# A copy of one column of zeros as ScalarE's first operation, in causal attention followed by a gated MLP

## The chip, the cores and the metric

The kernel runs on one core of one Trainium2 chip. The metric is the device time of the program in microseconds. A profile is one execution with the hardware profiler on; its span runs from the first to the last recorded work, and the execution's own time is a little longer.

## The reference

Attention over 8 batches, 8 heads, 576 positions and 64 values a head, with a mask that is causal by blocks of 64; then the heads are put side by side as `x` of 4608 x 512 and go through a gated MLP without an activation function:

```python
scores = scale * np.matmul(q, k.transpose(0, 1, 3, 2))     # scale = 1 / sqrt(64)
scores = np.where(block_i >= block_j, scores, -1000000000.0)
scores = scores - np.max(scores, axis=-1, keepdims=True)
attn = np.exp(scores)
attn = attn / (np.sum(attn, axis=-1, keepdims=True) + 1e-09)
attn_out = np.matmul(attn, v)
...
a = x @ w1
b = x @ w2
h = a * b @ w3
return h @ w_out
```

## The kernel before, in words

Two heads of one batch make a pair; there are 32 pairs (`NN`), and the transposed q and k of a pair fill 128 partitions, 64 for each head. The weights come as 64-bit numbers and are put together on the chip from two 32-bit halves (`assemble`, L161 to L172: one ScalarE operation, L168, then three VectorE operations, L169 to L171). The products `w3 @ w_out` are formed once on the chip (`gen_product`, L461), so that the MLP has two stages: the gated one (L481) and the output one (L499).

The work falls into three parts. The opening (L124 to L529) prepares the first pair. Pairs 0 to 3 (`EARLY`) run attention while the weights arrive, are put together and multiplied; their score tiles are L281, their exponentials L289, their products with v L321. From pair 4 on, attention of one pair runs interleaved with the MLP of the tokens that are finished, by hand-written orders (`FIRST_PLANS`, `PLAN`), one letter per step.

The opening goes like this. SP issues the loads of the first pair: k, then q (`load_qk(0)`, L116), the identity matrix (L129), v (L121), and the constants (L138). VectorE sets a tile `cst` of 128 x 1152 to zero (L135), and the two DMAs of L138 write five rows of constants into each half of it. `shift_mask(0)` (L189) casts k to bf16 (`kb`, L192) and q into the block-diagonal `qd` in two halves, the first on VectorE and the second on ScalarE (L194). TensorE then forms bf16 scores from the two (`mx`, L206), VectorE takes their row maxima (`m`, L213), TensorE transposes them (`mt`, L217), ScalarE negates them (`ms`, L219), and SP writes them as rows into the operand tiles `qk` (`shift`, L228). Meanwhile ScalarE casts q and k into `qk` (L251), SP copies them to the other half of the partitions (L255), ScalarE copies zeros and constants from `cst` into the rest of `qk` (L521), SP fetches the first piece of weights (`wraw`, L158), and VectorE forms the low parts (L258). Then the first score tiles (L281) can run.

What sets the order: inside the opening, `manual_schedule` holds PE, VectorE, ScalarE, SP and GpSimd to the order of the program. For pairs 0 to 3 a planner in the framework orders each engine's instructions by priority and its own estimate of times; the attention steps have high priority, the weights fill in. From pair 4 on TensorE's order is the program's. Each engine and each queue works in order. Waits between engines come from the data that the instructions read and write, tile region by tile region. The table load of ScalarE is not in the source: the compiler puts it in ahead of an operation.

Of the kernel before, what the change touches and what calls it, by code (L numbers as in the profile page):

```python
# [7 lines left out]
F32 = mybir.dt.float32  # L8
# [8 lines left out]
P = 128  # L17
# [60 lines left out]
def block_causal_attention__then__gated_mlp_kernel(ctx, tc, qkv, consts, ident_in, w1, w2, w3t, wout, out_t):  # L78
    nc = tc.nc
    w1, w2, w3t, wout = (w.bitcast(I32) for w in (w1, w2, w3t, wout))  # L80

    cpool = ctx.enter_context(tc.tile_pool(name="cpool", bufs=1))
# [50 lines left out]
    tl["early"] = wp  # L133
    cst = wp.tile([P, RQK], F32, tag="rqk", name="cst")
    nc.vector.memset(cst, 0.0)  # L135
    five = [slice(oth[j].start, oth[j].start + 5) for j in range(2)]
    for j in range(2):
        nc.sync.dma_start(out=cst[five[j]], in_=consts)  # L138
# [513 lines left out]
```

## Time and profile before

| | before |
|---|---|
| median of three runs | 965.94 us (965.72 to 966.31) |
| the profiled execution's own time | 964.53 us |
| its span | 962.7 us |
| mean granted TensorE clock | 0.995 of full speed |
| TensorE, VectorE, ScalarE, GpSimd busy | 97%, 63%, 59%, 32% of the span |
| DMA | 111.68 MB, mean 116 GB/s |

Times in the profile are microseconds from the start of the span. PE is TensorE, PEld its weight loads, DVE VectorE, ACT ScalarE, POOL GpSimd, SP the engine that issues the DMAs; a name with q (SPq, ACTq) is an engine's sequencer. A row names a line of the kernel, the operation, the tile written, the tile read, the shape and a count; in brackets stands how long the engine was idle before it and who ended that. The chain of waits is followed back from the last instruction: at each step to what released it.

### The profile page before, as it was taken

The numbers are of one execution on the slowest core, as the hardware profiler recorded it, in microseconds if no ns is written. First come the engines' busy times: TensorE is split into PE (matmuls) and PEld (weight loads), VectorE is DVE, ScalarE is ACT, GpSimd is POOL, SyncE is SP. The second block draws the span as 40 slices with busy tenths as digits, with TensorE's granted clock in tenths as the row PEclk, the third lists the DMA queues.
The fourth block names the chain that finished last, engine by engine and source line by source line (L and its number), as shares of the span: only waits on it lengthen the run. The fifth ranks groups of instructions, "written<-read, shape, count | busy, mean of one in ns | idle before, by whom it ended". The sixth has DMA issues, their size and how long they took to land.

```text
span 962.7 us, 13385 instructions
## 1 busy us (share of the span) xinstructions
PE 936.8 (97%) x4608; PEld 750.4 (78%) x4608; DVE 608.7 (63%) x1289; ACT 565.4 (59%) x1274; POOL 304.4 (32%) x254
## 2 busy tenths in 40 slices
PE   5799979999999999999999999999999999999998
PEld 3355557888888888888888888888888888888886
DVE  5999977766777667766776777767776776210010
ACT  5677666666666666666666667666666665222121
POOL 0000043443345334533443334333443443223120
PEclk9999979999999999999999999999999999999999
DMA  7797333455444554455445544554454442000001
GB/s 255 248 296 236 136 82 94 113 124 145 113 113 114 144 124 113 107 143 118 109 100 142 123 109 112 133 130 107 108 130 125 108 114 60 22 1 33 12 1 44
DMA packets 48823, 111.68 MB, mean 116 GB/s; under 512 B 5866, under 2 KB 14186, under 8 KB 48756
## 3 DMA queue, kind: packets, MB, share of 16 engines
q1 hardware_dynamic: 48756, 110.84, 44.3%
q8 instruction: 36, 0.59, 0.3%
q14 instruction: 31, 0.25, 0.1%
HBM read 50.51 MB, written 9.44 MB: 62 GB/s over the span
## 4 chain that ended last, share of the span: by engine, by line
PE 90%; ACT 4%; DVE 3%; DMA 1%; issue 1%; SPq 0%; POOL 0%; ACTq 0%
PE ab L481 41%; PE o L499 20%; PE s L281 10%; PE x L345 9%; PE mx L206 4%; PE w L461 3%; PE x L321 2%; DMA rqk<-in_qkv 1%; ACT wbits L168 1%; DMA wraw<-in_wout 1%; DVE wbits L170 1%; ACT qk L251 1%; PE tot L362 0%; ACT x L371 0%; PE mt L217 0%
## 5 line engine op out<-in xcount | busy, mean ns | idle before, releaser
L489 POOL TENSOR_TENSOR gl<-a,gh 128x512 fp32r<-128x512 f32 x72 | 93.6, 1300 | 238.7 <-ACT gh L488 238.7
L281 PE MATMUL s<-qk 128*128 128x288 f32 (+4 forms) x768 | 159.8, 313 | 8.7 <-DMA qk<-ms 5.7
L281 PEld LDWEIGHTS s<-qk 128*128 128x128 f32 (+1 forms) x768 | 125.8, 183 | 40.7 <-issue 9.9
L213 DVE TENSOR_REDUCE m<-mx 128x1 f32<-128x512 f32 (+6 forms) x256 | 125.9, 504 | 36.2 <-PE mx L206 34.8
L300 ACT ACTIVATE ph<-s 128x448 fp32r<-128x448 f32 x224 | 86.1, 384 | 70.3 <-PE s L281 63.4
L481 PE MATMUL ab<-xh,w2h 128*128 128x512 f32 x288 | 126.6, 440 | 0.0
L271 POOL TENSOR_TENSOR vs<-rv,vs 128x320 fp32r<-128x320 f32 x56 | 48.8, 871 | 235.5 <-ACT vs L270 235.5
L499 PE MATMUL o<-gh,wh 128*128 128x512 f32 x288 | 117.3, 407 | 0.0
L487 DVE TENSOR_TENSOR a<-ab,a 128x512 f32<-128x512 f32 x72 | 49.6, 689 | 106.7 <-PE ab L481 104.0
L302 DVE TENSOR_TENSOR pl<-s,ph 128x448 fp32r<-128x448 f32 x168 | 81.6, 485 | 54.3 <-ACT s L301 53.8
L481 PE MATMUL ab<-xh,w1h 128*128 128x512 f32 x288 | 114.5, 398 | 0.1
L481 PE MATMUL ab<-xl,w1h 128*128 128x512 f32 x288 | 113.6, 394 | 0.0
L298 DVE TENSOR_TENSOR pl<-rsum,ph 128x288 fp32r<-128x288 f32 x112 | 56.3, 526 | 90.4 <-ACT ph L297 90.2
L481 PE MATMUL ab<-xh,w1l 128*128 128x512 f32 x288 | 113.2, 393 | 0.0
L481 PE MATMUL ab<-xl,w2h 128*128 128x512 f32 x288 | 113.1, 393 | 0.0
L499 PE MATMUL o<-gl,wh 128*128 128x512 f32 x288 | 112.8, 392 | 0.0
L481 PE MATMUL ab<-xh,w2l 128*128 128x512 f32 x288 | 112.8, 392 | 0.0
L499 PE MATMUL o<-gh,wl 128*128 128x512 f32 x288 | 112.6, 391 | 0.0
L243 POOL TENSOR_TENSOR rqk<-rqk,hf 128x1152 fp32r<-128x1152 f32 x27 | 72.2, 2675 | 91.1 <-ACT hf L240 82.6
L303 DVE TENSOR_TENSOR rsum<-s,rsum 128x448 f32<-128x448 f32 x224 | 92.9, 415 | 1.7
L345 PE MATMUL x<-ph,vs 128*128 128x128 f32 x336 | 87.3, 313 | 0.2 <-DVE ph L302 0.2
L301 ACT ACTIVATE s<-s 128x448 f32<-128x448 f32 x224 | 85.7, 382 | 0.0
(76 smaller groups left out, 1743.6 us busy)
## 6 DMA issues: line engine op xcount, KB each, us to landing
qk<-hf SPq DMA_DIRECT2D x108, 288.0 KB, 3.1
rqk<-in_qkv SPq DMA_DIRECT2D x31, 576.0 KB, 4.8
qk<-rqk SPq DMA_DIRECT2D x54, 288.0 KB, 4.8
rv<-in_qkv SPq DMA_DIRECT2D x32, 320.0 KB, 2.8
out_t<-o SPq DMA_DIRECT2D x36, 256.0 KB, 2.0
wraw<-in_w3t SPq DMA_DIRECT2D x8, 1024.0 KB, 6.1
wraw<-in_w SPq DMA_DIRECT2D x8, 1024.0 KB, 7.6
wraw<-in_wout SPq DMA_DIRECT2D x4, 1024.0 KB
```

The costliest lines, as they stand in the source:

```text
L213: nc.vector.reduce_max(m[:, col : col + 1], sc, axis=AX.X)
L243: nc.gpsimd.tensor_tensor(out=lo, in0=rqk_of[n], in1=hf, op=ALU.subtract)
L281: nc.tensor.matmul(t[ks, at : at + q1 - q0], qk[j][:, 2 + s, kr], qk[j][:, s, q0:q1], start=(s == 0), stop=(s == 1))
L298: nc.vector.tensor_tensor(out=low, in0=r, in1=h, op=ALU.subtract)
L300: nc.scalar.activation(h, sc, AF.Exp, scale=SCALE)
L301: nc.scalar.activation(sc, sc, AF.Exp, scale=SCALE)
L302: nc.vector.tensor_tensor(out=low, in0=sc, in1=h, op=ALU.subtract)
L303: nc.vector.tensor_tensor(out=r, in0=sc, in1=r, op=ALU.add)
L345: nc.tensor.matmul(xps[:, to : to + w], v[:, c, :], parts[s][:, a : a + w], start=(u < 2 and s == 0), stop=((u, s) in ((0, 1), (len(PV) - ...
L481: nc.tensor.matmul(acc[i], l[:, c, fs], r[c], start=(c == 0 and s == 0), stop=(c == NC - 1 and s == 2))
L489: nc.gpsimd.tensor_tensor(out=gl[f // 4][:, f % 4], in0=a32, in1=gh[f // 4][:, f % 4], op=ALU.subtract)
L499: nc.tensor.matmul(t, l[:, f, es], r[f // 4][:, f % 4], start=(f == 0 and s == 0), stop=(f == NF - 1 and s == 2))
```

## The change

After the memset of `cst`, ScalarE copies its first column (128 partitions, one element each) into a new tile of one column in the pool `cpool`, which nothing reads. The line stands ahead of the two DMAs that write the constants into `cst`, and ahead of every other ScalarE operation of the program.

```diff
@@ -133,6 +133,7 @@
     tl["early"] = wp
     cst = wp.tile([P, RQK], F32, tag="rqk", name="cst")
     nc.vector.memset(cst, 0.0)
+    nc.scalar.copy(cpool.tile([P, 1], F32, name="table"), cst[:, 0:1])
     five = [slice(oth[j].start, oth[j].start + 5) for j in range(2)]
     for j in range(2):
         nc.sync.dma_start(out=cst[five[j]], in_=consts)
```

## The prediction

> **What bounds the kernel now.** I read the page first, for the engine that fills the span and for the chain that ended last.
>
> ```profile
> span 962.7 us, 13385 instructions
> PE 936.8 (97%) x4608; PEld 750.4 (78%) x4608; DVE 608.7 (63%) x1289; ACT 565.4 (59%) x1274; POOL 304.4 (32%) x254
> PE 90%; ACT 4%; DVE 3%; DMA 1%; issue 1%; SPq 0%; POOL 0%; ACTq 0%
> ```
>
> The reader is to see that TensorE is the kernel: busy for 97% of the span and 90% of the chain. A change to one ScalarE operation can only matter where the chain leaves TensorE. So the next view was the chain of waits, from the start to 30 us.
>
> ```profile
> 0.74 0.40 SPq L116
> ...
> 1.19 3.12 DMA rqk<-in_qkv
> ...
> 4.33 0.02 ACTq L194
> ...
> 4.39 1.28 ACT L194
> ...
> 5.68 0.67 ACT qd L194
> ...
> 8.72 0.60 SPq L255
> ...
> 9.37 5.68 DMA wraw<-in_wout
> ...
> 15.07 1.13 ACT wbits L168
> ...
> 16.55 1.11 PE s L281 x2
> ...
> 18.36 1.49 PE x L321 x2
> ...
> 21.69 0.43 PE mx L206 x2
> ...
> 27.59 0.75 PE x L321 x2
> ```
>
> Columns are start, duration, what. The first 16 us hold no TensorE link at all. The first pair's q and k land at 1.19 + 3.12 = 4.31, ScalarE passes its semaphore at 4.33, and then 1.28 us go to something on line 194 that is not yet the cast of qd: that begins at 5.68. The timeline of the same stretch says what it is.
>
> ```profile
> 1.04 1.02 DVE L135 MEMSET cst<- 128x1152 f32 x1 [1.04 <-PEq L640]
> ...
> 2.60 0.69 SPq L138 DMA_DIRECT2D cst<-in_consts  x2
> ...
> 4.39 1.28 ACT L194 ACT_TABLE_LOAD   x1 [4.39 <-DMA rqk<-in_qkv]
> 4.41 0.74 DVE L194 CAST qd<-rqk 64x576 bf16<-64x576 f32 x1 [0.37 <-DMA rqk<-in_qkv]
> 5.68 0.67 ACT L194 CAST qd<-rqk 64x576 bf16<-64x576 f32 x1
> ...
> 6.40 1.04 PE L206 MATMUL mx<-kb,qd 128*128 128x512 bf16 x2 [6.40 <-ACT qd L194]
> ...
> 7.55 1.77 SPq L255 DMA_DIRECT2D qk<-qk  x2
> ...
> 8.60 2.32 ACT L521 CAST qk<-cst 64x1152 fp32r<-64x1152 f32 x2
> ...
> 11.50 0.27 ACT L219 ACTIVATE ms<-mt 9x128 fp32r<-9x128 f32 x1 [0.57 <-PE mt L217]
> ...
> 15.37 0.82 PE L281 MATMUL s<-qk 128*128 128x288 f32 x2 [2.18 <-DMA qk<-ms]
> ...
> 18.16 1.70 PE L321 MATMUL x<-pe,ve 128*128 128x448 f32 x2
> ...
> 21.53 0.59 PE L206 MATMUL mx<-kb,qd 128*128 128x512 bf16 x2
> ...
> 27.43 0.92 PE L321 MATMUL x<-pe,ve 128*128 128x448 f32 x2
> ```
>
> It is an ACT_TABLE_LOAD that stands behind the wait for the data. ScalarE did nothing in the 4.39 us before, and the load stands in full on the path that releases TensorE's first matmul at 6.40.
>
> **The change part by part.** *The added copy.* It reads one column of cst, so it waits for the memset, which ends at 1.04 + 1.02 = 2.06. No row shows a copy of 128x1. The nearest small ScalarE row is ms at 0.27 us for 9x128; one element a partition should not be dearer, and an instruction costs not less than nothing, so 0 to 0.27, and I take 0.27, as that row is small already. Behind it on ScalarE's queue stands everything else of that engine, none of which can start before the data. In the late case the load waits for the memset as it now waits for the data: 2.06 + 1.28 + 0.27 = 3.61. In the early case the load stands ahead of the wait and the copy ends at 2.06 + 0.27 = 2.33. Both are before 4.31, with 0.70 us to spare in the worse. The cover is ScalarE's idle time; if it were gone, the copy would cost its 0.27 at most.
>
> *The load that moves.* Line 194's cast on ScalarE can begin where the load began, at 4.39, instead of 5.68: 1.29 us earlier. It then ends at 4.39 + 0.67 = 5.06. What is late next is VectorE's half of qd, at 4.41 + 0.74 = 5.15: TensorE needs both. Its first matmul came 0.05 after the ScalarE half (5.68 + 0.67 = 6.35, then 6.40), so it comes at 5.20, and that path gains 1.20. The other path, the two casts of L251, the two DMAs of L255 and the first weight fetch behind them on SP, gains the whole 1.29: the fetch goes out at 9.37 - 1.29 = 8.08 and lands near 13.8, where ScalarE takes it up for wbits. The paths meet at about 16 us: TensorE's second score tile (15.37, behind the row of maxima) carries 1.20, ScalarE's wbits (15.07) carries 1.29. The later one counts: 1.20.
>
> A page speaks for more than this: the Trainium skill, page "ScalarE: Activation LUTs", section "What ACT_TABLE_LOAD costs", gives 1283 ns for the load and some 1380 ns of drain, 2.66 us per switch. The trace agrees with the load alone: the cast starts 0.01 us after it ends. By the page the sum would be 2.66.
>
> All that stands between the landing and the cast is 5.68 - 4.31 = 1.37, so the direct gain has that for its upper end. Its lower end is zero, if the load does not move.
>
> *The wait that is added.* The copy reads all 128 partitions of column 0 of cst, and the two DMAs of L138 then write ten rows of it, that column too. They must now wait for the copy. They went out at 2.60; now at 2.60 (early case) or 3.61 (late case). Behind them on SP's queue stands nothing until L255, at 7.55 before and 6.26 now, and two issues at 0.69 together end at 4.30: SP is not held up. Who needs the constants is L521, at 8.60 before and 7.31 now. Landing time for 22.5 KB is not shown; the nearest row is the far larger load of rqk, 0.74 to 4.31, 3.57 us from issue. By that they land at 4.30 + 3.57 = 7.87 at worst, 0.56 late; the 0.57 us that ScalarE stands idle before ms hides this. Cost nothing; if the cover is gone, 0.56.
>
> The new tile of one column adds bytes to a pool but no instruction. Other queues are not passed.
>
> *Whether it lasts to the end.* Everything from 6.40 on waits for something that came from this first chain, not for a fixed time, so it moves as a block.
>
> ```profile
> 50.00:66.00 16.00, 16.00 (x58) 8.62 (x58) 16.00 (x22) 11.74 (x19) 0.00 (x0) 1.00 0.86 268
> ...
> 200.00:300.00 100.00, 100.00 (x535) 84.31 (x534) 68.91 (x162) 65.03 (x158) 39.41 (x33) 1.00 0.49 119
> ```
>
> In these windows (from:to, length, then busy time of PE, weight loads, VectorE, ScalarE, GpSimd, clock, DMA share, GB/s) TensorE is busy throughout: work that starts earlier is done earlier, and there is no gap that could take the gain back. Sum: -1.20, within -1.37 and 0.
>
> The profiled execution took 964.53 us, its span of 962.7 and 1.83 around it. From it the change gives 963.33. The three timed runs have their median at 965.94, 1.41 above, and as the forecast is for such runs I put 965.94 - 1.20 = 964.74, say 964.7. About 0.2%, 1.93 us, is what a measurement of this kernel can tell from no change: the forecast is below that.
>
> **The rivals.** *The clock at the start* (faster or less fast). On the chain the two products of 448 columns at 18.36 took 1.49 us, those at 27.59 0.75 (the timeline's rows from 18.16 and 27.43 give the form), and the two 512-column products at 21.69 took 0.43 against 1.04 at 6.40. So TensorE ran at half speed until shortly before 21.69. If the rise to full speed stays where it is in absolute time, the 1.20 us won are half-speed time and worth 0.60: 965.3. If it comes earlier by more than the work does, the half-speed stretch in which the chain is TensorE's, from 16.55 to 21.69, shrinks; at the most all of its 5.14 us halve, another 2.57: between 964.0 (where 0.2% begins) and 962.2, some 963.1. Against a large effect speaks that the three runs lie within 0.6 us of each other.
>
> The Trainium skill, page "TensorE: Matmul & The Clock Gate", section "What's actually happening", says that the activity window of 3413 ns runs freely and is not restarted by the kernel. By that rule the rise does not follow the work, and each run would draw its own share; the close times of the runs do not bear that out.
>
> *The other clock dip* (faster).
>
> ```profile
> 130.00:140.00 10.00, 8.50 (x26) 6.59 (x26) 7.31 (x9) 6.19 (x15) 4.88 (x4) 0.51 0.31 93
> ```
>
> Where the stage of the first four pairs ends, the granted clock is 0.51. Should the shifted schedule avoid it, TensorE's 8.50 busy us halve, 4.25 less: 960.5. It has no reason to: what precedes it moves as a block.
>
> *The drain counts too* (faster). A second 1.38 behind the load would go too: 965.94 - 2.66 = 963.3. The 0.01 us between load and cast speaks against it.
>
> *No load moves, or there are two* (same). If the load is placed by the first operation that really needs a table, or one set serves the copy and another Abs and Exp, the first cast or wbits still waits 1.28. For one set for all:
>
> ```profile
> L194 ACT ACT_TABLE_LOAD x1 | 1.3, 1283 | 4.4 <-DMA rqk<-in_qkv 4.4
> ```
>
> Before, one load in the whole run came ahead of a cast and served exponentials too. Price: 965.9.
>
> *The planner orders the early pairs otherwise* (slower). After the opening, the orders of VectorE, ScalarE and SP in the first four pairs come from a planner's estimates, and an added ScalarE operation shifts them. The place is a weight piece put ahead of a mask or a low part that TensorE waits for.
>
> ```profile
> L168 ACT ACTIVATE wbits<-wraw x20: 1129/1158/1227, 15.1 to 110.9; 128x1024 f32<-128x1024 f32 x20
> L169 DVE TENSOR_SCALAR wbits<-wbits x20: 653/690/695, 16.2 to 118.0; 128x1024 int32<-128x1024 int32 x20
> L170 DVE SCALAR_TENSOR_TENSOR wbits<-wraw,wbits x20: 1171/1218/1226, 17.0 to 119.3; 128x1024 int32<-128x1024 int32 x20
> L171 DVE SCALAR_TENSOR_TENSOR w<-wraw,wbits x8: 1216/1218/1225, 27.7 to 96.7; 128x1024 int32<-128x1024 int32 x8
> ```
>
> One piece is 1.16 + 0.69 + 1.22 + 1.22 = 4.29 us from ScalarE to VectorE. In front of TensorE it costs 4.29 - 1.20 = 3.09: 969.0. It decides from 3.13 us of new waiting on (1.20 + 1.93). Against it: the copy lies ahead of the first data and moves no estimate that the data set.
>
> **How the numbers follow.** The block shift of 1.20 (964.7): 0.66. Rise of the clock unmoved (965.3): 0.08. Rise earlier still (963.1): 0.10. No gain from the load (965.9): 0.07. Planner (969.0): 0.06. Other dip (960.5): 0.02. Drain (963.3): 0.01. Faster by over 0.2%: 0.10 + 0.02 + 0.01 = 0.13. Slower by as much: 0.06. The same: 0.81. The range goes from 963.2 (the drain case and about half of the earlier rise are in) to 966.2 (no gain, and 0.3 for the spread of the three runs); about 0.13 is left out.
>
> **What would show it.** In the profile after, the table load begins before 2.4 us and there is one of it; the copy of one column ends by 3.61; L194's cast on ScalarE begins at 4.39 and TensorE's first matmul at 5.20, now released by VectorE; the consts' DMAs go out by 3.6 and L521 starts near 7.3; the first weight fetch goes out at 8.1; the order on every engine is as before, and at 200 us all stands 1.2 earlier. The forecast is wrong if the load stays behind the data, if TensorE's first fast matmuls do not come 1.2 earlier, or if a wait between 16 and 130 us appears that was not there.

## The result and the profile after

The changed kernel is slower: 972.85 us, median of six runs (972.45 to 974.57), against 965.5 us for the kernel before beside it (six runs, 961.86 to 966.31). The ratio is 1.0087, 95% interval 1.0077 to 1.0097. The profiled execution took 973.0 us, its span is 971.2. In the code after, the copy is L136, and every line behind it has a number one higher (L195 is the former L194).

The timeline of the opening, after:

```profile
0.73 1.28 ACT L136 ACT_TABLE_LOAD   x1 [0.73 <-PEq L641]
...
2.10 0.19 ACT L136 COPY table<-cst 128x1 f32<-128x1 f32 x1
...
2.60 0.68 SPq L139 DMA_DIRECT2D cst<-in_consts  x2
...
4.42 0.67 ACT L195 CAST qd<-rqk 64x576 bf16<-64x576 f32 x1 [2.13 <-DMA rqk<-in_qkv]
4.43 0.74 DVE L195 CAST qd<-rqk 64x576 bf16<-64x576 f32 x1 [0.35 <-DMA rqk<-in_qkv]
...
5.33 1.01 PE L207 MATMUL mx<-kb,qd 128*128 128x512 bf16 x2 [5.33 <-DVE qd L195]
...
7.34 2.32 ACT L522 CAST qk<-cst 64x1152 fp32r<-64x1152 f32 x2
```

The table load starts with the engine, at 0.73; the copy runs at 2.10, and ScalarE's cast no longer waits for anything but its data. TensorE starts at 5.33 instead of 6.40, released by VectorE's half. The chain of waits after, with the same links as in the prediction:

```profile
4.36 0.02 ACTq L195
...
4.42 0.67 ACT qd L195
...
8.11 5.81 DMA wraw<-in_wout
...
13.94 1.13 ACT wbits L169
...
15.42 1.11 PE s L282 x2
...
17.23 1.49 PE x L322 x2
...
20.53 0.43 PE mx L207 x2
```

The first weight fetch goes out at 8.11 instead of 9.37; the second score step starts at 15.42 instead of 16.55; the fast row-maximum products come at 20.53 instead of 21.69. So far the forecast holds, with 1.1 to 1.3 us won. The loss comes later, and steadily. SP's issues of the first output tile of a block of tokens, in block one and in block six, of the kernel before and then of the changed one (start, duration, line):

```profile
213.12 0.35 SPq L504 DMA_DIRECT2D out_t<-o  x1
...
707.30 0.35 SPq L504 DMA_DIRECT2D out_t<-o  x1
```

```profile
212.45 0.36 SPq L505 DMA_DIRECT2D out_t<-o  x1
...
711.21 0.35 SPq L505 DMA_DIRECT2D out_t<-o  x1
```

At block one the changed kernel is still 0.67 us ahead; five blocks later it is 3.91 behind. That is 4.58 us in five blocks, 0.92 a block, and a block has 288 products of 512 columns in the MLP: 3.2 ns a product, if all of it is theirs. The last stretch of the chain shows it without attention beside it. Before, then after:

```profile
893.60 5.44 PE ab L481 x24
899.08 38.37 PE ab L481 x168
937.46 21.77 PE o L499 x96
```

```profile
900.17 5.60 PE ab L482 x24
905.80 39.47 PE ab L482 x168
945.27 22.41 PE o L500 x96
```

The same 288 products take 5.60 + 39.47 + 22.41 = 67.48 us instead of 65.58. An output product follows the one before it after 22.41 / 96 = 233 ns instead of 21.77 / 96 = 227. TensorE waits for nobody in either; it streams more slowly. Two such blocks cost 3.8 us, seven blocks at 0.92 some 6.4, together 10.2; less the 1.1 of the opening that is 9.1, by this rough sum, where the spans differ by 8.5 us. TensorE's weight loads follow the same order of tiles in both traces, and so do the instructions of the other engines but for the added copy, so no planner's decision is in it.

### The profile page after: what moved, and what is told of

It reads as the page before. It is cut to its first block, busy times and chain, and to the rows that moved or that the text cites. A ratio compares the mean times of both kernels' runs of the same rounds, so it can differ in the third digit from the quotient of the medians.

```text
span 971.2 us, 13356 instructions
## 1 busy us (share of the span) xinstructions
PE 946.2 (97%) x4579; PEld 750.1 (77%) x4608; DVE 608.8 (63%) x1289; ACT 566.1 (58%) x1275; POOL 304.1 (31%) x254
## 4 chain that ended last, share of the span: by engine, by line
PE 90%; DVE 4%; ACT 3%; DMA 2%; issue 1%; SPq 0%; ACTq 0%
PE ab L482 42%; PE o L500 21%; PE s L282 10%; PE x L346 9%; PE mx L207 3%; PE w L462 2%; PE x L322 2%; DVE wbits L171 1%; DMA wraw<-in_w3t 1%; ACT qk L252 1%; DMA wraw<-in_wout 1%; ACT wbits L169 1%; DVE w L172 1%; PE tot L363 0%; DVE m L214 0%
## 5 line engine op out<-in xcount | busy, mean ns | idle before, releaser
L489 ACT CAST gh<-a 128x512 fp32r<-128x512 f32 x72 | 44.3, 616 | 70.3 <-DVE a L488 69.0
```

## The experiments

What the diff does besides the copy: its tile stands behind the weights, identity, `qk` and `qd` in the pool `cpool`, so everything that is allocated later starts 32 bytes (a tile's smallest size in a partition) further on. Among that are `xh`, `xl`, `gh` and `gl`, the moving operands of the MLP. The first theory was that TensorE reads operands more slowly when they start off a round address (A, a multiple of 64); the rivals were the copy or the moved load itself (B), the old place itself or a multiple of 128 (C), and the places of the work tiles. All ratios are to the kernel before on the same chip; its medians in the three sets of four runs are 963.95, 964.91 and 963.9 us. An edit is shown against the changed kernel unless it says otherwise.

**The tile 64 bytes long.**

```diff
-    nc.scalar.copy(cpool.tile([P, 1], F32, name="table"), cst[:, 0:1])
+    nc.scalar.copy(cpool.tile([P, 16], F32, name="table")[:, 0:1], cst[:, 0:1])
```

> The changed kernel, but the tile that the copy writes is 64 bytes a partition long instead of 32 (16 columns, the copy writes the first), so every later tile starts 64 bytes further on than before, at a multiple of 64 again. Theory A (TensorE reads its moving operands more slowly when they start 32 bytes off a multiple of 64, 227 against 234 ns from one 512-column product to the next in the last stretch): the loss is gone and the 1.2 us of the opening stay, so about 1.2 us under the kernel before, 964.3 if that is 965.5. Theory B (the added copy, or the other place of the table load, slows TensorE in some way): as the changed kernel, 972.9. Theory C (what counts is a multiple of 128 or the old place itself): 972.9 too, with late tiles at 64 past a multiple of 128.

Measured: 967.63 us, ratio 1.0039 (1.0027 to 1.0050). Between the expectations: over half of the loss is gone, not all. The last 96 output products, from the chain:

```profile
940.05 21.99 PE o L500 x96
```

21.99 / 96 = 229 ns. B and C, which left all of the loss, are weakened, and A in its simple form is wrong.

**The tile without the copy.**

```diff
-    nc.scalar.copy(cpool.tile([P, 1], F32, name="table"), cst[:, 0:1])
+    cpool.tile([P, 1], F32, name="table")
```

> The kernel before with the tile of one column taken from the pool and nothing that writes it: no copy, the table load behind the data as before, every later tile 32 bytes further on. Theory A: the loss without the gain of the opening, 965.5 + 7.4 + 1.2 = about 974, and 234 ns between products at the end. Theory B: as the kernel before, 965.5. Theory C as A.

Measured: 973.65 us, ratio 1.0101 (1.0088 to 1.0114).

```profile
4.38 1.28 ACT L195 ACT_TABLE_LOAD   x1 [4.38 <-DMA rqk<-in_qkv]
```

```profile
946.87 22.41 PE o L500 x96
```

The table load is back behind the data, nothing is computed that was not before, and the pace is the changed kernel's. B is out: 32 bytes of allocation make the loss.

**The late operands put back to a multiple of 64.**

```diff
+        pool.tile([P, 1], F32, name="pad")
         tl["ph"] = pool.tile([P, PW], F32R, name="ph")
```

The pad is the first tile of the pool `late`.

> The changed kernel with 32 bytes left free at the start of the pool that holds the moving operands of the MLP (xh, xl, gh, gl), ph, pl and vs, so that these stand at multiples of 64 again; the loads of q, k and v, kb, x32 and the other work tiles stay 32 bytes off. Theory A, if it is the MLP's and the attention products' operands alone: about 964.3, as with the tile of 64 bytes. If the work tiles that VectorE, ScalarE, GpSimd and the DMAs use matter, most of the 8 us stay: 970 or more. Theory B: 972.9.

Measured: 967.03 us, ratio 1.0039 (1.0024 to 1.0054), runs from 964.43 to 969.11 us; the last 96 output products take 21.99 us again:

```profile
937.14 21.99 PE o L501 x96
```

`kb`, `x32` and the loads of q, k and v still stand 32 bytes off here, and it is no slower than with 64 bytes everywhere. So the work tiles cost nothing that shows; the late pool carries the loss. Its profiled run has a span of 962.7 us, the kernel before's, with a shorter clock dip (last section), so it isn't compared by its span.

**Only `gh` and `gl` 32 bytes off, on the kernel before.**

```diff
+        pool.tile([P, 1], F32, name="pad")
         tl["gh"] = [pool.tile([P, 4, TB], F32R, name=f"gh{h}") for h in range(2)]
```

> The kernel before, without the copy, with 32 bytes left free ahead of gh and gl: only the moving operands of the output products (gh, gl; behind them a32, o32 and hf) start 32 bytes off. Theory A: of the 288 products of 512 columns in a block of tokens the 96 of the output stage alone are slower, by 3.3 ns in the seven blocks beside attention and by 6.5 in the last two: 2.2 + 1.2 = 3.4 us more, 969; in the last stretch 96 output products take 22.4 us and the 168 of the gated stage still 38.4. Theory B: 965.5.

Measured: 968.04 us, ratio 1.0044 (1.0032 to 1.0056), 4.1 us at the medians where 3.4 were expected.

```profile
902.16 38.37 PE ab L482 x168
940.53 22.42 PE o L500 x96
```

The output products alone are slower, the gated ones beside them are not: it is a matter of each product's own operands.

Since 64 bytes gave 229 ns, a second theory about the start modulo 128 bytes (A2) stood against a theory about the distance between the weights that a product loads and the operand that it streams (D). Four runs tell them apart.

**The copy in place, no tile.**

```diff
-    nc.scalar.copy(cpool.tile([P, 1], F32, name="table"), cst[:, 0:1])
+    nc.scalar.copy(cst[:, 0:1], cst[:, 0:1])
```

> The copy with no new tile: it reads the first column of the zeroed constants and writes it back in place. Every tile stands where it stood before the change. Theory A2 (TensorE's products depend on where their moving operands start, modulo 128 bytes: 227 ns from product to product at 0, about 229 at 64, 233 at 32) and theory D (on how far the moving operands stand from the weights): nothing is lost and the opening's 1.2 us are won, so 1.2 us under the kernel before, 227 ns in the last stretch. Theory B (the copy or the moved table load slows TensorE): about 973.

Measured: 963.12 us against 964.91, ratio 0.9981 (0.9971 to 0.9991).

```profile
938.38 21.77 PE o L500 x96
```

The table load is at 0.73 and the last output products take what they took before the change. This is what the prediction priced.

**Weights 32 bytes off, moving operands at multiples of 128, on the kernel before.**

```diff
+    cpool.tile([P, 8], F32, name="pad0")
     both = cpool.tile([P, 2 * P], F32, name="ident")
...
     qd = cpool.tile([P, NB, P], BF16, name="qd")
+    cpool.tile([P, 24], F32, name="pad1")
```

> The kernel before, without the copy, with 32 bytes left free ahead of the first tile and 96 behind the last tile of the pool that holds the weights: weights, identity, qk and qd start 32 bytes off a multiple of 64, all later tiles (the moving operands of the MLP among them) 128 bytes further on, at multiples of 128. Theory A2 (moving operands alone): the MLP's products as before, 227 ns; only the score products and the row-maximum products, whose moving or stationary operands stand in that pool, can be slower; 965 to 966. If the stationary operands count as well, or theory D (the distance from weights to moving operands, now 96 more): slower by several us, 970 or more.

Measured: 976.84 us, ratio 1.0123 (1.0110 to 1.0136), the highest of all, though the interval overlaps with that of the tile without the copy.

```profile
949.21 22.42 PE o L501 x96
```

The distance from weights to moving operands is 96 bytes longer here.

**Everything 32 bytes off, on the kernel before.**

```diff
+    cpool.tile([P, 1], F32, name="pad0")
     both = cpool.tile([P, 2 * P], F32, name="ident")
```

> The kernel before, without the copy, with 32 bytes left free ahead of the first tile: every tile, weights and moving operands alike, 32 bytes further on, so that the distances between them stay. Theory A2: as with the tile alone, about 973.7 and 233 ns, or somewhat more, as the score products are moved too. Theory D: as the kernel before, about 964, 227 ns.

Measured: 965.2 us against 964.91, ratio 1.0001 (0.9991 to 1.0011).

```profile
937.96 21.77 PE o L500 x96
```

The moving operands stand exactly where they stand in the changed kernel, and nothing is lost, because the weights moved too. A and A2 fall, and of C the old place; D holds.

**The tile 128 bytes long**, as the first experiment with 32 columns:

> The changed kernel, with the tile that the copy writes 128 bytes a partition long, so that all later tiles are 128 bytes further on. Theory A2: at multiples of 128 again, so 227 ns in the last stretch and 1.2 us under the kernel before. Theory D, or if the old places themselves were the good ones: slower than the kernel before, as with 64 bytes (1.0039 of it) or worse.

Measured: 970.96 us, ratio 1.0069 (1.0056 to 1.0082).

```profile
941.60 22.32 PE o L500 x96
```

A round start does not help; 128 bytes more distance cost 22.32 / 96 = 232.5 ns a product. Then the period, and a way to keep the diff's own tile.

**The tile 256 bytes long** (64 columns).

> The changed kernel, with the tile that the copy writes 256 bytes a partition long, so that the moving operands of the MLP stand 256 bytes further from the weights. Theory D (TensorE's pace from product to product depends on the distance between the weights that it loads and the moving operands that it streams, modulo some power of two), with a period of 256 bytes: as the copy in place, 227 ns and 0.998 of the kernel before. With a period of 512: another distance not tried yet (0 instead of 256, modulo 512), at which the pace can be anything from 227 to 235 ns. Theory A2 (start of the moving operands alone, modulo 128) is ruled out by the runs before.

Measured: 962.66 us against 963.9, ratio 0.9991 (0.9982 to 1.0000), 21.77 us for the last output products. 256 bytes more distance cost nothing.

**The diff's own tile, taken first.**

```diff
+    table = cpool.tile([P, 1], F32, name="table")
     both = cpool.tile([P, 2 * P], F32, name="ident")
...
-    nc.scalar.copy(cpool.tile([P, 1], F32, name="table"), cst[:, 0:1])
+    nc.scalar.copy(table, cst[:, 0:1])
```

> The change as it is, with its tile of 32 bytes and its copy, but the tile is taken from the pool ahead of the weights instead of behind them: every tile is 32 bytes further on, all distances are as before. Theory D: 227 ns in the last stretch and the opening's 1.2 us won, 0.998 of the kernel before, as with the copy in place. A theory in which the place of a tile itself counts: as the changed kernel, 1.0087.

Measured: 963.41 us, ratio 0.9994 (0.9985 to 1.0003), 21.77 us again. The loss is gone; the gain is not clear of zero in this run alone.

**The tile 512 bytes long** (128 columns).

> The changed kernel, with a tile of 512 bytes a partition. The weights of neighbouring products lie 512 bytes apart, so a distance that is 512 bytes longer is met by the same products again. Theory D with a period of 256 or 512: 227 ns, 0.998 of the kernel before. If it is slower, the period is longer than 512, or it is not the distance.

Measured: 962.45 us, ratio 0.9986 (0.9976 to 0.9995), and 21.77 us once more.

**TensorE alone.** This kernel leaves out the reference's computation.

```diff
+    for step in range(-2, 41):
+        words = 8 * max(step, 0)
+        acc = psum.tile([P, 512], F32, tag="acc", name="warm" if step < 0 else "d" + "abcdefghijklmnopqrstuvwxyzABCDEFGHIJKLMNO"[step])
+        for i in range(24):
+            nc.tensor.matmul(acc, w[:, i % 4 * P : (i % 4 + 1) * P], mov[:, words : words + 512], start=(i == 0), stop=(i == 23))
```

> Not the reference's computation: all of it is left out. TensorE alone, 24 products of 512 columns (fp32r, weights 128x128 in four slices 512 bytes apart) for each of 41 distances between weights and moving operand, from 0 to 1280 bytes past a multiple of 512 in steps of 32; the accumulators are called da, db and so on. No other engine works beside. Theory D: the pace changes with the distance, 227 ns at 256 past, 233 at 288, 231 at 384 and up to 237 at 352, and repeats after 256 or 512 bytes. If the pace is the same at all distances, it takes other engines' work to make the loss, and theory D falls in this form.

The chain, one line for 24 products at each distance, 32 bytes more from line to line (da: a multiple of 256; di and dq: 256 and 512 more):

```profile
19.03 5.44 PE da L97 x24
24.47 5.60 PE db L97 x24
30.08 5.50 PE dc L97 x24
35.58 5.61 PE dd L97 x24
41.19 5.60 PE de L97 x24
46.79 5.62 PE df L97 x24
52.41 5.60 PE dg L97 x24
58.01 5.60 PE dh L97 x24
63.61 5.47 PE di L97 x24
69.07 5.60 PE dj L97 x24
74.68 5.50 PE dk L97 x24
...
108.21 5.46 PE dq L97 x24
```

With no other engine at work, the pace is 5.44 / 24 = 227 ns at a multiple of 256 bytes, 5.50 / 24 = 229 at 64 past it, and 233 to 234 at every other multiple of 32; it repeats every 256 bytes. The numbers of the whole kernel are the same to within a nanosecond: 227, 229, 232.5, 233. The expectation had the period right and two sizes wrong: 233 instead of 231 ns at 128 past a multiple of 256 (de), and 234 at most instead of 237. In the kernel before, all distances of the MLP happen to be multiples of 256 (by the tile sizes added up in the program's order, `xh` starts 641 x 256 bytes behind `w1h`, and `gh` 597 x 256 behind `wh`).

## Why the prediction was wrong, step by step

The opening was right in mechanism and nearly in size. The load left the path in the early case; the copy took 0.19 us where 0.27 was allowed; the constants' DMAs were not delayed (2.60). The weight fetch came at 8.11 (8.08 forecast), L522 at 7.34 (7.31). TensorE's first product came at 5.33 rather than 5.20, as it followed VectorE's half by 0.16 us and not by the 0.05 carried over. The four kernels that keep the distances (modulo 256) and move the load lie at 0.9981, 0.9991, 0.9994 and 0.9986 of the kernel before, 0.6 to 1.8 us under it, around the forecast 1.20.

In this trace the rise to full speed moved with the work: the fast products came at 20.53, 1.16 earlier, 5.11 us behind the second score step, where the kernel before had 5.14. That is not so in every trace. With the copy in place they came 4.37 us behind that step (19.77 after 15.40), with the tile of 256 bytes 5.75 (21.16 after 15.41), so the rival of a clock that rises at another moment is real, though smaller than the loss here. The rise is read from the products' pace alone: in both traces the granted clock is 1.00 in every stretch from 12 to 27 us.

What failed is the sentence "The new tile of one column adds bytes to a pool but no instruction", and with it "it moves as a block". The bytes were costed at nothing without looking at what stands behind them in memory. Between the two spans that missing term is 8.5 + 1.1 = 9.6 us. At 213 us only 0.67 was left of the 1.2 that was to stand at 200. The windows in which TensorE is busy throughout were read as safe, since there is no gap to lose; but a stage that is TensorE's alone passes on every nanosecond of its products' pace, and 3.2 ns by 288 products by seven blocks (6.4 us) is more than the whole gain. None of the rivals had this mechanism. The planner's rival, priced at 969.0, had the right direction by luck: no order changed. It was luck too that the three runs before, on which the argument against a large effect of the clock leaned, lay within 0.6 us: the six beside the changed kernel cover 4.5.

The Trainium skill, page "SBUF — State Buffer", section "Who interferes with whom", gives TensorE two independent read ports, one for the moving operand and one for weight loads, and says that TensorE waits on nobody. With no other engine at work, the traces show what that section does not mention: the pace of these products depends on how far the two operands lie apart, 227 against 233 ns.

Shown is the dependence on the distance, by moving either operand and both. That the next product's weight load collides with the current stream is an inference: no run left the weight loads away. The loss beside attention is 3.2 ns a product, and 6.6 (1.90 us by 288) without it. Part of that is seen in 18 output products that follow each other beside attention, of the kernel before and then of the changed one:

```profile
427.35 4.13 PE o L499 x18
```

```profile
428.57 4.20 PE o L500 x18
```

They take 229 ns each before and 233 after. The changed kernel's products are as slow as alone, while those of the kernel before, 227 ns alone, have already lost some of their pace there. Why they lose it beside attention is not shown.

## What to carry to other kernels

A new tile, however small, moves all that is allocated after it; where TensorE is the bound, compare the pace of the products in the last, undisturbed stretch (time by count in the chain) before crediting or blaming anything else. Keep the distance between weights and moving operands what it was: write into existing bytes, take the new tile ahead of both, or pad it to 256 bytes. This is shown for fp32r products of 512 columns with weights of 128 x 128, and for no other type. Moving an ACT_TABLE_LOAD (1.28 us) that stands behind the first data was worth about a microsecond here, once, by giving ScalarE a first operation that waits for something earlier.

## What the runs showed of the hardware that was not expected

Apart from the pace, the clock dip near 130 us is not the same in every trace. Windows of the tile of 512 bytes and of the late operands put back, with the granted clock in the third column from the end:

```profile
130.00:134.00 4.00, 3.27 (x10) 2.17 (x8) 3.92 (x4) 2.76 (x7) 4.00 (x4) 0.64 0.73 223
134.00:138.00 4.00, 3.19 (x17) 2.83 (x18) 2.71 (x5) 2.44 (x6) 0.44 (x1) 1.00 0.01 2
```

```profile
130.00:134.00 4.00, 2.52 (x9) 2.03 (x10) 3.93 (x5) 1.89 (x6) 2.86 (x3) 0.82 0.41 137
134.00:138.00 4.00, 4.00 (x23) 3.46 (x23) 1.75 (x5) 3.90 (x8) 0.00 (x0) 1.00 0.00 0
```

Both are back at 1.00 by 134, while the kernel before was at 0.51 from 130 to 140, and the copy in place at 0.50 from 134 to 138. Executions of one kernel on one chip lie up to 4.7 us apart (961.98 to 966.66 for the kernel before in the last set, with mean granted clocks of 0.998 and 0.989), which is why a microsecond took a dozen runs to see.
